# Zero matmuls in the idle time of TensorE, in a planned attention kernel with 32-row score matmuls

## The chip, the cores and the metric

The kernel runs on one core of a Trainium2 chip. The metric is the device time of one execution in microseconds, from the first to the last work on that core. Two runs of the kernel before are shown. The core has five engines that the text names by the profile's short names: PE (TensorE, matrix multiplication; PEld is its weight load), DVE (VectorE), ACT (ScalarE), POOL (GpSimd) and SP (SyncE, which issues the DMAs here).

## The reference: what is computed

The input x has 2048 tokens of 512 values in bfloat16. Four layers follow each other, A, B, A, B, each of them added to x, and each fed with a layer norm of x. A and B have their own weights, which both of their uses share.

```python
def _A_ref(x, wq, wk, wv, wo):          # 32 heads of 16, one key and one value head
    q = (x @ wq).reshape(B, S, H, Dh)   # per head
    k = x @ wk; v = x @ wv
    scores = einsum("bhqd,bkd->bhqk", q, k) * (Dh ** -0.5)
    o = einsum("bhqk,bkd->bhqd", softmax(scores), v)
    return o.reshape(B, S, H * Dh) @ wo

def _B_ref(x, wqkv, wo):                # linear attention, 32 heads of 16
    pq, pk = phi(q), phi(k)             # phi(t) = (t + 1 if t > 0 else exp(t)) + 1e-6
    kv = einsum("bhsd,bhse->bhde", pk, v); z = pk summed over s
    o = einsum("bhqd,bhde->bhqe", pq, kv) / (einsum("bhqd,bhd->bhq", pq, z) + 1e-6)
    return o.reshape(B, S, D) @ wo
```

The bulk of the work is A: for each of 32 heads a score matrix of 2048 by 2048, its exponential, and a product with 16 columns of values and one column of ones that gives the sum for the softmax.

## The kernel before, in words

**Scores.** A head has only 16 values, so a score matmul contracts over 16. The kernel gives it 32 rows of TensorE: queries of eight heads lie on the 128 partitions of `QT`, and the keys are repeated eight times down the partitions of `Kr`, in two copies. Copy `par` keeps the 16 rows of the even or the odd heads and has zeros in the others (`mpar` is the mask). A score matmul for head pair `j` (0 to 3) then reads the 32 partitions from 32 j on, of copy `par` and of the queries, and gives the scores of 128 keys by 512 queries of one head in one accumulator bank (`smm`, L569). Three score matmuls at different j can run side by side in TensorE.

**Positions.** The work of one A layer is a list of 2048 positions: a unit is a block of 512 queries, a group of eight heads and a copy (32 units), and a unit has 16 key tiles times 4 values of j. Each position is taken by one of two routes.

- The ACT route (`fill`, L668): three positions at a time, three score matmuls into one of two sets of three banks, one exponential by ACT over 1536 columns into a buffer of `PTA` (L689), then value matmuls.
- The DVE route (`dstep` and `dpass`, L704 and L744): one score matmul into bank 6, DVE turns it into an integer form (`xT`, L735); after two of them six DVE steps over 1024 columns make the exponential from the bits (`xu`, `xs`, L751 to L755) into a buffer of `PTD` (L756). This route works at least `LEAD` = 26 positions ahead.

**Values.** For each position four matmuls of 17 columns (`add_pv`, L583, issued at L608) use the exponentials as weights and add to columns 0 to 271 of bank 7. A unit has 64 such groups in bank 7. When the last is planned, DVE takes the reciprocal of the sums (`rden`, L620) and multiplies (`Osb`, L625). Bank 7 passes to the next unit after that. After the second copy of a head group, `Osb` is transposed (L793), copied to `OT` and, with all groups of a block, projected with `wo` and added to x.

**Mixed work.** When a block of 512 tokens of A is done, its layer norm, the B projections (`b_prep`, L823, all through the helper `proj`, L475) and `phi` are run while attention goes on with the next block. The rest of B (`b_main`, L876) runs tile by tile when A has ended, and in the first half of the kernel it is mixed with the projections for the next A.

**What sets the order.** Nothing is ordered by hand. A planner (`Sched`) runs a small model of the engines when the program is built. Each operation has a planned duration per engine, a priority, its inputs and the buffers it takes and gives back; whenever an engine is free in planned time (`run`, L180), the ready operation of best priority is appended to that engine's queue. Planned durations are for example 0.06 + 0.08 per score matmul (a set: 0.30 us), 0.22 for a score matmul of the DVE route, 0.15 for four value matmuls, 0.09 + 0.000833 per column for ACT (1.37 us for 1536), and 0.03 + 0.00036 per column for a projection matmul. The result is one fixed queue per engine, with semaphore waits where an operation needs another engine's result. On the chip nothing is reordered between the queues.

Buffers that the change touches: `NPA`, `NPD` (PTA and PTD, six each), `NE` (three exponentials of `phi`), `NO2` (three tiles in `b_main`).

Of the kernel before, what the change touches and what calls it, by code (L numbers as in the profile page):

```python
# [44 lines left out]
class Sched:  # L45


    def __init__(self, nc):
        self.nc = nc
        self.now = 0.0  # L50
        self.engs = [PE, AC, DV, PO, SP]
        self.tfree = {e: 0.0 for e in self.engs}
        self.pend = {e: [] for e in self.engs}
        self.ready = {e: [] for e in self.engs}
        self.order = {e: [] for e in self.engs}
        self.events = []
        self.seq = 0
        self.lastw = {}
        self.readers = {}
        self.all = []  # L60
        self.step = lambda now: False
        self.act_ok = lambda op: True
        self.ndma = 0

# [115 lines left out]
    def run(self):  # L180
        while True:
            go = True
            while go:
                go = self.step(self.now)
                for e in self.engs:
                    if self.tfree[e] <= self.now + 1e-9 and self._try(e):
                        go = True
            if not self.events:
                break
            t, _, f = heapq.heappop(self.events)  # L190
            self.now = max(self.now, t)
            if f is not None:
                f()
            while self.events and self.events[0][0] <= self.now + 1e-9:
                _, _, f = heapq.heappop(self.events)
                if f is not None:
                    f()
        left = [o for e in self.engs for (_, _, o) in self.ready[e] + self.pend[e] if not o.done]
        assert not left, [(o.name, o.engs) for o in left[:20]]
        STATS["end"] = max(o.vis for o in self.all)  # L200
# [112 lines left out]
def bass_interleave_layers__grouped_kv_mqa__linear_attn_block__prompt_kernel(  # L313
# [17 lines left out]
    LEAD = 26  # L331
    KC = 2

    xv = A_x.rearrange("b (t p) d -> p (b t) d", p=P)
# [6 lines left out]
    xnT = sb("xnT", [P, FT, S], BF16)  # L341
    NXN, NE = 3, 3
    xn_buf = sb("xn_buf", [P, NXN, D], BF16)
# [7 lines left out]
    mask8 = sb("mask8", [P, 8, 17], FP32)  # L351
    mpar = sb("mpar", [P, 2], FP32)
    wq_sb = sb("wq_sb", [P, FT, D], BF16)
# [6 lines left out]
    QT = sb("QT", [P, 2, NG, 512], BF16)  # L360
    Kr = sb("Kr", [P, 2, S], BF16)
    Vaug = sb("Vaug", [P, T, 20], BF16)
    NPA, NPD, NDX = 6, 6, 2
    PTA = sb("PTA", [P, NPA, 1536], BF16)
# [3 lines left out]
    xs = sb("xs", [P, NDX, 1024], FP16)  # L368
    Osb = sb("Osb", [P, 2, 4, D], BF16)
    OT = sb("OT", [P, 2, NG, 4, P], BF16)  # L370
# [7 lines left out]
    kvzbd = sb("kvzbd", [P, NG, 8 * 17], BF16)  # L378
    NO2 = 3
    Osb2 = sb("Osb2", [P, NO2, D], BF16)  # L380
# [31 lines left out]
    for c, (a, b) in enumerate(((0, 2), (2, 4), (4, 8), (8, 12), (12, 16))):  # L412
# [3 lines left out]
        if c == 1:  # L416
# [14 lines left out]
                                           fill=0.0, base=DH, channel_multiplier=-1), writes=["mask"], prio=1)  # L431
    add(DV, 0.1, lambda e: e.tensor_reduce(out=mpar[:], in_=mask8[:, :, 0:1].rearrange("p (a b) c -> p b (a c)", b=2),
                                           axis=mybir.AxisListType.X, op=ALU.add), reads=["mask"], writes=["mpar"], prio=2)
# [5 lines left out]

    state = {"layer": -1, "ctl": None}  # L440

# [40 lines left out]
    def k_proj(L, t0, n, prio):  # L482
        h = H_()
        a, b = t0 * P, (t0 + n) * P
        o = proj(h, [(wk_rep[:, ft, :], xnT[:, ft, a:b]) for ft in range(FT)], b - a, ["wkrep"] + [("xnT", t) for t in range(t0, t0 + n)], prio, name="kp")
        for m in range(2):
            def ev(e, m=m):
# [3 lines left out]
            if m == 0:  # L491
                ops = {}
            ops[m] = add((DV, AC), {DV: tdv(b - a), AC: tac(b - a)}, ev, deps=[o] + ([ops[0]] if m else []), uses=[h], rel=[h] if m else [],
                         reads=["mpar"], writes=[("K", m, t) for t in range(t0, t0 + n)], prio=prio - 0.05, name="kev")
# [32 lines left out]
    class Ctl:  # L527
# [25 lines left out]
        def ok(self, p):  # L553
            u, kt, j = self.pos[p]
            qb, g, par = self.units[u]
            a = self.have.get(("K", self.layer, par, kt))
            b = self.have.get(("Q", self.layer, qb, g))
            return a is not None and b is not None and a.done and b.done and a.vis <= sc.now + 0.05 and b.vis <= sc.now + 0.05
# [10 lines left out]
        def smm(self, e, p, b):  # L569
            u, kt, j = self.pos[p]  # L570
            qb, g, par = self.units[u]
            return e.matmul(bank(b), lhsT=Kr[32 * j:32 * j + 32, par, kt * P:(kt + 1) * P],  # L572
                            rhs=QT[32 * j:32 * j + 32, qb % 2, g, :], start=True, stop=True)

        def keys(self, ps_):
            r = []
            for p in ps_:
                u, kt, j = self.pos[p]
                qb, g, par = self.units[u]
                r += [("K", par, kt), ("QT", qb % 2, g)]  # L580
            return list(dict.fromkeys(r))

        def add_pv(self, p, src, hold, dep, last):  # L583
# [21 lines left out]
            def f(e):  # L605
                first = opened[0]
                for qs in range(4):
                    i = e.matmul(bank(7, 17, (qs * 4 + j) * 17), lhsT=src(qs), rhs=Vaug[:, kt, 0:17],  # L608
                                 start=(first and qs == 0), stop=(qs == 3), skip_group_check=True)
# [4 lines left out]
        def norm(self, u, last):  # L614
# [5 lines left out]
            o = add(DV, 0.246, lambda e: e.reciprocal(rden[:, hr.idx, :].unsqueeze(2), av[:, :, DH:DH + 1]), deps=[last], acq=[hr], uses=[h7], prio=0.0, name="recA")  # L620
            c0 = (8 * g + par) * DH
            ov_ = Osb[:, qb % 2, :, 128 * g:128 * (g + 1)].rearrange("p s (j r d) -> p s j r d", j=4, r=2)[:, :, :, par, :]

            def ml(e):
                return e.tensor_tensor(out=ov_, in0=bank(7, 272).rearrange("p (s j c) -> p s j c", s=4, j=4)[:, :, :, 0:DH],  # L625
                                       in1=rden[:, hr.idx, :].rearrange("p (s j) -> p s j", s=4).unsqueeze(3).to_broadcast([P, 4, 4, DH]), op=ALU.mult)
            o = add(DV, tdv(256), ml, deps=[o], uses=[h7, hr], rel=[h7, hr], writes=[("Osb", qb % 2, g, par)], prio=-0.01, name="mulA")
# [3 lines left out]
        def step(self, now):  # L631
            if self.layer is None:
                return False
            if self.ramp and all(self.have.get(("K", self.layer, m, t)) is not None and self.have[("K", self.layer, m, t)].done
                                 for m in range(2) for t in (0, T - 1)):
                self.ramp = False
# [4 lines left out]
            if self.pa >= n:  # L641
                self.tail = True
                self.layer_done()
                return False
# [59 lines left out]
        def dstep(self):  # L704
# [4 lines left out]
            while self.pd < n and self.taken[self.pd]:  # L709
                self.pd += 1  # L710
            if self.pd >= n or not self.ok(self.pd):
                return False
# [31 lines left out]
        def dpass(self, c):  # L744
            hx, hp = c["hx"], c["hp"]
            k = hx.idx
            lo = xT[:, k, :].bitcast(U16).rearrange("p (n two) -> p n two", two=2)[:, :, 0]
            pr = 3.0
            u_, s_ = xu[:, k, :], xs[:, k, :]
            kw = dict(uses=[hx], prio=pr)  # L750
            o = add(DV, tdv(1024, 0.52), lambda e: e.tensor_scalar(out=u_, in0=lo, scalar1=1.0 / 65536, scalar2=-0.5, op0=ALU.mult, op1=ALU.add), deps=c["p1"] + c["prev"], name="xu", **kw)  # L751
            o1 = add(DV, tdv(1024, 0.52), lambda e: e.tensor_tensor(out=s_, in0=u_, in1=u_, op=ALU.mult), deps=[o] + c["prev"], name="xsq", **kw)  # L752
            o2 = add(DV, tdv(1024, 0.26), lambda e: e.tensor_scalar(out=s_, in0=s_, scalar1=XK, scalar2=-XW, op0=ALU.mult, op1=ALU.add), deps=[o1], name="xw", **kw)  # L753
            o3 = add(DV, tdv(1024, 0.26), lambda e: e.tensor_scalar(out=u_, in0=u_, scalar1=1.0, scalar2=XL, op0=ALU.mult, op1=ALU.add), deps=[o1], name="xl", **kw)  # L754
            o4 = add(DV, tdv(1024, 0.52), lambda e: e.tensor_tensor(out=s_, in0=s_, in1=u_, op=ALU.mult), deps=[o2, o3], name="xc", **kw)  # L755
            o5 = add(DV, tdv(1024), lambda e: e.scalar_tensor_tensor(out=PTD[:, hp.idx, :].bitcast(U16), in0=xT[:, k, :], scalar=2.0 ** -9, in1=s_, op0=ALU.mult, op1=ALU.add),  # L756
                     deps=[o4] + c["prev"], uses=[hx, hp], rel=[hx], prio=pr, name="xo")
# [17 lines left out]

        def layer_done(self):
            if self.dcur is not None:
                raise AssertionError("open batch")

    ctl = Ctl()  # L780
    sc.step = ctl.step
    sc.act_ok = lambda op: ctl.ramp or ctl.tail
    banks.sets_for_misc = lambda: (1, 0) if (ctl.tail or (ctl.ramp and not (ctl.layer is not None and ctl.ok(0)))) else ((1,) if ctl.ramp else ())


    def epi_tr(L, qb, g):
# [3 lines left out]
        def tr(e):  # L790
            v = bank_bf(h.idx)
            for qs in range(4):
                i = e.transpose(v[:, qs, :], Osb[:, qb % 2, qs, g * P:(g + 1) * P], ident[:])  # L793
            return i
# [190 lines left out]
```

The softmax here doesn't subtract the row's maximum and nothing guards it: scores larger than these inputs give would overflow.

## Time and profile before

| | us |
|---|---|
| runs before | 1939.4 and 1934.91, median 1937.16 |
| the profiled execution | 1937.57, of which 1935.7 in the span from its first to its last instruction |
| exponentials by ACT (L689), 1179 of them | 1625.1 busy, 1464 ns each |
| score matmuls (L572), 4096 of 32 rows by 512 columns | 914.0 busy, 582 ns each |
| value matmuls (L608), 16384 of 17 columns, 14144 of them from PTA | 584.0 busy (PTA), 176 ns each |
| first DVE step (L735), 560 | 385.1 busy, 688 ns each |
| last DVE step (L756), 280 | 340.5 busy, 1216 ns each |
| mean granted clock of TensorE | 0.575 |

Durations are those of one profiled execution. Matmuls overlap each other, so a group's busy time is less than its count times its mean, and the time from one matmul's start to the next one's start says more than a duration. The profile's row of granted clock tells, in tenths, which part of TensorE's full clock its throttle let through: 1.0 is full and 0.5 half, and the records hold no other value here. "Idle before" is time in which an engine had nothing to do just before an instruction, with the engine that ended it.

By time, the span has these parts: the first layer norms, projections and a growing attention to about 50 us; attention of the first A to 900, from about 270 on with B's projections in it; the rest of B and the next projections to 1000; attention of the second A to about 1850, from about 1200 on with projections; the rest of the last B and the output to 1936.

### The profile page before, as it was taken

To read this page: it belongs to the slowest core of one execution; us is meant where nothing else is said; L and a number is where in the kernel's file an instruction comes from. 1 tells how busy PE (TensorE), PEld (TensorE's weight loads), DVE (VectorE), ACT (ScalarE), POOL (GpSimd) and SP (SyncE) were. 2 spreads that over 40 slices of the span, in tenths; PEclk is the share of its full clock that TensorE was granted. 3 is DMA by queue.
4 is the path that set the end of the run, shared out by engine and by line. 5 is a ranking of instruction groups with operands and counts; after the bars stand their busy time and mean duration, and the time that the engine had idled before them with its cause. 6 is when DMAs were issued, how large, how long until landed. Compare 5 with 4: busy or idle time off the path is not lost.

```text
span 1935.7 us, 49030 instructions
## 1 busy us (share of the span) xinstructions
PE 1778.2 (92%) x22208; PEld 820.9 (42%) x22208; DVE 1712.9 (88%) x3063; ACT 1702.0 (88%) x1330; POOL 45.1 (2%) x77
## 2 busy tenths in 40 slices
PE   7999999999999999998889999999999999997977
PEld 4444444444444444443444444444444444443434
DVE  7899989999889988887879999899898989985977
ACT  6999999999989999997589999999998999986973
POOL 2000000000000000000100000000000000000000
PEclk8555556555665555555975555655565555556559
DMA  3000000000000000000000000000000000000001
GB/s 110 2 1 2 2 1 2 2 2 2 1 2 2 2 1 2 2 2 2 1 2 2 2 2 2 2 2 2 1 2 1 2 1 2 2 2 1 2 1 44
DMA packets 7808, 10.50 MB, mean 5 GB/s; under 512 B 1456, under 2 KB 7088, under 8 KB 7600
## 3 DMA queue, kind: packets, MB, share of 16 engines
q1 hardware_dynamic: 7600, 7.37, 1.2%
q8 instruction: 173, 2.83, 0.6%
q14 instruction: 35, 0.29, 0.0%
HBM read 5.28 MB, written 2.10 MB: 4 GB/s over the span
## 4 chain that ended last, share of the span: by engine, by line
PE 57%; DVE 29%; ACT 11%; issue 1%; DMA 0%; POOL 0%; SPq 0%
PE ps_all L572 27%; PE ps_all L608 16%; PE ps_all L475 11%; ACT PTA L689 10%; DVE xT L735 8%; DVE PTD L756 6%; DVE xu L751 3%; DVE xs L755 2%; DVE xs L752 2%; DVE xu L754 1%; DVE xs L753 1%; PE ps_all L920 1%; DVE stats L444 1%; PE ps_all L458 1%; DVE x_sb L931 1%
## 5 line engine op out<-in xcount | busy, mean ns | idle before, releaser
L689 ACT ACTIVATE PTA<-ps_all 128x1536 bf16<-128x1536 f32 x1179 | 1625.1, 1464 | 117.7 <-PE ps_all L572 108.8
L572 PE MATMUL ps_all<-QT,Kr 32*128 32x512 bf16 x4096 | 914.0, 582 | 80.0 <-ACT PTA L689 38.8
L608 PEld LDWEIGHTS ps_all<-Vaug,PTA 128*128 128x128 bf16 x14144 | 470.3, 104 | 566.0 <-issue 552.6
L608 PE MATMUL ps_all<-Vaug,PTA 128*128 128x17 bf16 x14144 | 584.0, 176 | 4.6 <-ACT PTA L689 2.5
L735 DVE TENSOR_SCALAR xT<-ps_all 128x512 int32<-128x512 f32 x560 | 385.1, 688 | 116.1 <-PE ps_all L572 105.1
L756 DVE SCALAR_TENSOR_TENSOR PTD<-xT,xs 128x1024 uint16<-128x1024 int32 x280 | 340.5, 1216 | 1.1
L572 PEld LDWEIGHTS ps_all<-QT,Kr 32*128 32x128 bf16 x4096 | 160.0, 98 | 311.6 <-ACT PTA L689 152.6
L751 DVE TENSOR_SCALAR xu<-xT 128x1024 f16<-128x1024 uint16 x280 | 192.3, 687 | 3.1
L755 DVE TENSOR_TENSOR xs<-xs,xu 128x1024 f16<-128x1024 f16 x280 | 191.0, 682 | 1.4
L752 DVE TENSOR_TENSOR xs<-xu 128x1024 f16<-128x1024 f16 x280 | 190.4, 680 | 0.5
L608 PE MATMUL ps_all<-Vaug,PTD 128*128 128x17 bf16 x2240 | 111.6, 176 | 16.6 <-DVE Osb L625 8.0
L753 DVE TENSOR_SCALAR xs<-xs 128x1024 f16<-128x1024 f16 x280 | 116.4, 416 | 1.0
L754 DVE TENSOR_SCALAR xu<-xu 128x1024 f16<-128x1024 f16 x280 | 117.0, 418 | 0.0
L608 PEld LDWEIGHTS ps_all<-Vaug,PTD 128*128 128x128 bf16 x2240 | 86.1, 104 | 66.8 <-DVE Osb L625 26.9
L475 PE MATMUL ps_all<-wqkv_sb,xnT 128*128 128x512 bf16 x256 | 106.3, 559 | 2.6 <-ACT xnT L464 1.4
L448 POOL TENSOR_TENSOR rstd<-veps,mhalf 128x1 f32<-128x1 f32 x64 | 40.9, 643 | 1842.2 <-DVE veps L446 1623.6
L815 ACT ACTIVATE e_buf<-ps_all 128x512 f32<-128x512 f32 x64 | 37.8, 597 | 39.8 <-PE ps_all L475 38.7
L475 PE MATMUL ps_all<-xnT,wq_sb 128*128 128x512 bf16 x128 | 55.8, 566 | 4.4 <-DVE xT L735 2.1
L475 PE MATMUL ps_all<-xnT,wqkv_sb 128*128 128x512 bf16 x128 | 52.4, 545 | 6.5 <-DVE pqT L818 5.6
L475 PE MATMUL ps_all<-wo_sb,OT 128*128 128x512 bf16 x128 | 51.9, 543 | 2.9 <-ACT OT L799 1.4
L444 DVE BATCH_NORM_STATS2 stats<-x_sb 128x6 f32<-128x512 bf16 x64 | 43.2, 683 | 3.5 <-DMA x_sb<-in_A_x_dram 3.3
L458 PE MATMUL ps_all<-ident,xn_buf 128*128 128x128 bf16 x256 | 31.2, 267 | 15.3 <-DVE xn_buf L451 13.6
(64 smaller groups left out, 625.9 us busy)
## 6 DMA issues: line engine op xcount, KB each, us to landing
out_dram<-x_sb SPq DMA_DIRECT2D x16, 128.0 KB, 1.7
x_sb<-in_A_x_dram SPq DMA_DIRECT2D x3, 512.0 KB, 7.3
wqkv_sb<-in_B_wqkv_dram SPq DMA_DIRECT2D x1, 1536.0 KB, 11.3
x_sb<-in_A_x_dram SPq DMA_DIRECT2D x2, 256.0 KB, 3.5
wq_sb<-in_A_wq_dram SPq DMA_DIRECT2D x1, 512.0 KB, 5.5
wo_sb<-in_A_wo_dram SPq DMA_DIRECT2D x1, 512.0 KB, 8.5
wo_sb<-in_B_wo_dram SPq DMA_DIRECT2D x1, 512.0 KB, 10.9
wk_sb<-in_A_wk_dram SPq DMA_DIRECT2D x1, 16.0 KB, 2.7
```

The costliest lines, as they stand in the source:

```text
L444: add(DV, tdv(512), lambda e: e.bn_stats(stats[:, t, 0:6], x_sb[:, t, :]), reads=[("x", t)], writes=[("st", t)], prio=prio, name="bn")
L475: i = e.matmul(bank(h.idx, n), lhsT=l, rhs=r, start=(c + k == 0), stop=(c + k == len(mms) - 1))
L572: return e.matmul(bank(b), lhsT=Kr[32 * j:32 * j + 32, par, kt * P:(kt + 1) * P], rhs=QT[32 * j:32 * j + 32, qb % 2, g, :], start=True, st ...
L608: i = e.matmul(bank(7, 17, (qs * 4 + j) * 17), lhsT=src(qs), rhs=Vaug[:, kt, 0:17], start=(first and qs == 0), stop=(qs == 3), skip_group_ ...
L689: oe = add(AC, tac(m * 512), lambda e: e.activation(PTA[:, hp.idx, 0:m * 512], bank(3 * s, m * 512), ACTF.Exp, scale=SCALE), deps=[o] + pr ...
L735: o = add(DV, tdv(512), lambda e: e.tensor_scalar(out=xT[:, hx.idx, i * 512:(i + 1) * 512], in0=bank(6), scalar1=SCALE * LOG2E * 65536.0, ...
L751: o = add(DV, tdv(1024, 0.52), lambda e: e.tensor_scalar(out=u_, in0=lo, scalar1=1.0 / 65536, scalar2=-0.5, op0=ALU.mult, op1=ALU.add), de ...
L752: o1 = add(DV, tdv(1024, 0.52), lambda e: e.tensor_tensor(out=s_, in0=u_, in1=u_, op=ALU.mult), deps=[o] + c["prev"], name="xsq", **kw)
L753: o2 = add(DV, tdv(1024, 0.26), lambda e: e.tensor_scalar(out=s_, in0=s_, scalar1=XK, scalar2=-XW, op0=ALU.mult, op1=ALU.add), deps=[o1], ...
L754: o3 = add(DV, tdv(1024, 0.26), lambda e: e.tensor_scalar(out=u_, in0=u_, scalar1=1.0, scalar2=XL, op0=ALU.mult, op1=ALU.add), deps=[o1], ...
L755: o4 = add(DV, tdv(1024, 0.52), lambda e: e.tensor_tensor(out=s_, in0=s_, in1=u_, op=ALU.mult), deps=[o2, o3], name="xc", **kw)
L756: o5 = add(DV, tdv(1024), lambda e: e.scalar_tensor_tensor(out=PTD[:, hp.idx, :].bitcast(U16), in0=xT[:, k, :], scalar=2.0 ** -9, in1=s_, ...
```

## The change

Score matmuls keep 32 rows. The change writes the row count as a parameter (`RG` = 32, from which `NRG` = 4 groups of rows and `NM` = 2 copies of the keys follow), adds matmuls that compute nothing, and makes several buffers smaller.

The added matmul has the identity as weights (128 rows by 128 columns) and a tile of zeros, 240 columns, as the moving operand. It adds to columns 272 to 511 of bank 7, which nobody reads. The planner adds one when TensorE is free in planned time after all ready work was tried, in the main part of attention only (not while an A layer ramps up, and not after its last position was taken), only while a unit has some but not all of its 64 value groups in bank 7, and only as far as a credit allows that grows by `DUMMY` = 0.25 us per planned us, up to 2.0, and pays 0.1 for each. It waits for nothing but the identity and the zeros.

```diff
+    RG = 32
+    NRG, NM = P // RG, RG // DH
+    DUMMY = 0.25
...
-    NXN, NE = 3, 3
+    NXN, NE = 3, 2
...
-    NPA, NPD, NDX = 6, 6, 2
+    NPA, NPD, NDX = 5, 5, 2
...
-    Osb = sb("Osb", [P, 2, 4, D], BF16)
+    Osb = sb("Osb", [P, 2, NG, 4, P], BF16)
...
-    NO2 = 3
+    NO2 = 2
...
+    zer = sb("zer", [P, 240], BF16)
+    add(PO, 0.3, lambda e: e.memset(zer[:], 0.0), writes=["zer"], prio=4)
```

In the planner's loop, after the engines were tried:

```diff
+            if self.tfree[PE] <= self.now + 1e-9 and self.events:
+                self.idle(self.now)
             if not self.events:
                 break
```

The new function:

```diff
+    credit = [0.0, 0.0]
+
+    def idle(now):
+        if ctl.layer is None or ctl.ramp or ctl.tail or DUMMY <= 0:
+            credit[0], credit[1] = 0.0, now
+            return
+        credit[0] = min(2.0, credit[0] + (now - credit[1]) * DUMMY)
+        credit[1] = now
+        u = ctl.acc_owner
+        if credit[0] < 0.1 or u < 0 or not 0 < ctl.count[u] < 64:
+            return
+        credit[0] -= 0.1
+        o = add(PE, 0.11, lambda e: e.matmul(bank(7, 240, 272), lhsT=ident[:], rhs=zer[:], start=False, stop=True, skip_group_check=True),
+                reads=["ident", "zer"], prio=9.0, name="dummy")
+        sc._try(PE)
+
+    sc.idle = idle
```

The score matmul and the place of its result in bank 7, in terms of the parameters:

```diff
-            return e.matmul(bank(b), lhsT=Kr[32 * j:32 * j + 32, par, kt * P:(kt + 1) * P],
-                            rhs=QT[32 * j:32 * j + 32, qb % 2, g, :], start=True, stop=True)
+            i, m = (j % NRG, par * (4 // NRG) + j // NRG)
+            r = slice(i * RG, (i + 1) * RG)
+            return e.matmul(bank(b), lhsT=Kr[r, m, kt * P:(kt + 1) * P], rhs=QT[r, qb % 2, g, :], start=True, stop=True)
...
-                    i = e.matmul(bank(7, 17, (qs * 4 + j) * 17), lhsT=src(qs), rhs=Vaug[:, kt, 0:17],
+                    i = e.matmul(bank(7, 17, (qs * 4 + (j % NRG) * (4 // NRG) + j // NRG) * 17), lhsT=src(qs), rhs=Vaug[:, kt, 0:17],
```

`Osb` is stored with the head group before the token tile, and its writer and reader (L625, L793) follow. At the end of a layer the DVE route may close a batch of one position instead of two; `dpass` then works on 512 columns instead of 1024:

```diff
-            if self.pd >= n or not self.ok(self.pd):
+            if self.pd >= n:
+                if self.dcur is not None:
+                    self.dpass(self.dcur)
+                    self.dcur = None
+                return False
+            if not self.ok(self.pd):
                 return False
```

The loops over the copies of the keys (mask, evictions, checks whether a key tile is there) run over `NM` instead of 2. Two unused names are removed.

## The prediction

> **What bounds the kernel now.** I read the page first: busy shares, the 40 slices, the chain.
>
> ```profile
> PE 1778.2 (92%) x22208; PEld 820.9 (42%) x22208; DVE 1712.9 (88%) x3063; ACT 1702.0 (88%) x1330; POOL 45.1 (2%) x77
> ...
> PE   7999999999999999998889999999999999997977
> ...
> ACT  6999999999989999997589999999998999986973
> ...
> PEclk8555556555665555555975555655565555556559
> ...
> PE 57%; DVE 29%; ACT 11%; issue 1%; DMA 0%; POOL 0%; SPq 0%
> ```
>
> Three engines are near full, and TensorE, which carries 57% of the chain, is granted about half its clock wherever attention runs. So I asked for the engines' busy time by stage.
>
> ```profile
> 100.00:250.00 150.00, 139.79 (x1872) 64.26 (x1871) 145.37 (x246) 144.87 (x105) 0.00 (x0) 0.50 0.01 2
> 250.00:900.00 650.00, 614.05 (x7803) 278.48 (x7800) 588.06 (x1019) 600.29 (x452) 11.07 (x12) 0.55 0.01 2
> ...
> 1050.00:1200.00 150.00, 137.68 (x1857) 64.33 (x1856) 142.50 (x242) 142.79 (x105) 0.00 (x0) 0.50 0.01 2
> 1200.00:1850.00 650.00, 608.37 (x7588) 272.65 (x7586) 574.90 (x998) 586.52 (x440) 7.88 (x12) 0.55 0.01 2
> ```
>
> Columns: stretch, length, then busy of PE, weight loads, DVE, ACT, POOL, then granted clock. Where attention runs alone (100 to 250) ACT and DVE are 96.6% and 96.9% busy: they bind, even at half clock. Where the next layer's projections are mixed in, they fall to 88 to 92%. The list of waits for 250 to 900 says for whom:
>
> ```profile
> DVE xT L735 <- PE ps_all L572: 40.3, 75, 1.9
> ...
> ACT PTA L689 <- PE ps_all L572: 36.6, 52, 1.5
> ```
>
> There TensorE is late, and its clock is what can be bought. What does the clock follow? Its records change only at multiples of 3.413 us; four windows on that grid:
>
> ```profile
> 286.99:290.40 3.41, 3.41 (x35) 1.35 (x32) 3.00 (x5) 3.27 (x3) 0.00 (x0) 0.50 0.00 0
> 290.40:293.81 3.41, 3.41 (x35) 1.30 (x33) 2.98 (x7) 2.04 (x3) 0.00 (x0) 0.50 0.02 5
> 293.81:297.23 3.42, 2.95 (x38) 1.08 (x36) 3.42 (x7) 3.42 (x3) 0.00 (x0) 1.00 0.00 0
> 297.23:300.64 3.41, 3.04 (x60) 1.90 (x61) 3.41 (x9) 3.41 (x4) 0.93 (x1) 1.00 0.00 0
> ```
>
> The first two are both 100% busy, yet only the second is followed by full clock. Count the columns that each matmul streams, times its rows over 128: the first has 4912 score columns of 32 rows (a quarter: 1228) and 24 value matmuls of 17 (408), 1636 in all. The second swaps score columns for 2293 full-row projection columns: 456 + 408 + 2293 = 3157. The third has 3491 and is followed by full clock, the fourth (10 score matmuls 1280, 46 value matmuls 782, four transposes 512) has 2574 and is followed by half. I did this count for all 568 windows of the trace: below 2900 none of 457 is followed by full clock, above 3200 all 50, between them 30 of 61. A threshold near 3000 misplaces 9 windows; counting the 32-row matmuls whole, whatever the other weights, misplaces at least 59. So the gate looks at rows in use, not at whether TensorE is busy.
>
> The Trainium skill ("TensorE: Matmul & The Clock Gate", Part 1) says that a window of sustained activity opens the gate and an idle one closes it. From 48.1 us on the clock stood at 0.5 for 211.6 us, with TensorE busy 187.90 of the 200.62 us from 59.38 to 260.00 and never idle for a whole window: the measurement decides. By the page's rule the added matmuls would have nothing to repair and be pure load, the 2455 us below.
>
> **The change, part by part.** *Renaming.* With 32 rows a group, NRG is 4 and NM is 2; rows, mask and accumulator columns come out as before. Osb is laid out anew, but the multiply still writes runs of 16 and the transposes still read 128 columns: 0.
>
> *Buffers.* PTA and PTD go from 6 to 5. A PTA buffer lives from its scores to its last value matmul, some 3 us by the rows (0.54 + 1.46 + 0.42 and handovers) against one new buffer per 1.43 us: three suffice. Osb2/OT2 go from 3 to 2. At the end a tile holds its pair about 3.6 us (reciprocal at 1901.36 to last matmul 1904.75, the next three alike) and tiles follow every 1.88 us; two pairs allow one per 1.8 to 1.9, so 0 to +6 us, I take 4. In the middle tiles follow every 3.4 us: 0. The exponential's buffer goes from 3 to 2, off attention's path since one bank serves it there: 0 to +2, I take 1. Together +5.
>
> *Zero tile and tail.* One POOL memset (the Vaug memset took 168 ns) at the start, on a queue busy 2%: ahead of the others it could delay the first rstd by 0.2 us. A half batch for DVE at a layer's end: at most one per layer, under 5 us either way, taken 0.
>
> *The zero matmuls, how many.* The planner gives 0.25 us of credit per planned us and takes 0.1 for each: 2.5 per us at most. It also needs planned idle time. Between 100 and 250 there are 372 scores per 105 exponentials, 3.54 each. Planned TensorE work per exponential is 0.30 + 3 x 0.15 + 0.54 x (0.22 + 0.15) = 0.95 of 1.37 us; the idle 0.42 holds 3.8 matmuls of 0.11 us, so credit binds: 3.4. From 250 to 900, 222 projection matmuls over some 420 exponentials take another 0.11, transposes 0.03: 2.5. Over the two layers about 1000 + 2100 = 3100 (2500 to 4100).
>
> *What one costs.* No trace row shows it. 512 columns are spaced 427 ns at half clock and 216 at full (projection rows), so 240 columns take 200 or 101 ns; the identity's weights load beside them as those of the value matmuls do (27 ns apart). Switching row shapes costs extra: value to score rows 108 ns against 27, projection to score 567 against 427. So 0.10 to 0.16 us at full clock; I take 0.10, as most will stand beside 128-row work. They wait for nothing after the start. Behind each are the score group that ACT or DVE waits for and the value matmuls that free PTA.
>
> *What the rest of TensorE gains.* A score group to the values behind it, then the same at full clock:
>
> ```profile
> 292.73 0.61 PE L572 MATMUL ps_all<-QT,Kr 32*128 32x512 bf16 x3
> ...
> 293.27 0.49 PE L608 MATMUL ps_all<-Vaug,PTA 128*128 128x17 bf16 x12
> ...
> 294.22 0.39 PE L572 MATMUL ps_all<-QT,Kr 32*128 32x512 bf16 x3
> ...
> 294.54 0.46 PE L608 MATMUL ps_all<-Vaug,PTA 128*128 128x17 bf16 x12
> ```
>
> 0.54 against 0.32 us; twelve value matmuls to the next scores are 0.42 against 0.39. Per exponential with its DVE share TensorE needs 1.23 us at half clock and 0.88 at full; with projections 1.46 and 1.00. Adding the zeros: at full clock 0.88 + 0.34 = 1.22 and 1.00 + 0.25 = 1.25, under ACT's 1.37 to 1.43. At half clock 1.23 + 0.68 = 1.91 and 1.46 + 0.50 = 1.96, over it: TensorE would bind.
>
> *Does the gate stay open?* Attention's windows from 62 to 250 held 1789 on average (spread 329). At full clock and the pitch 1.40 the zeros add 3.4 x 240 x 3.413 / 1.40 = 1990: 3780, over the threshold by more than twice the spread. With projections 2175 (spread 535) + 1460 = 3640, and more as work moves faster. Once open it holds. Once shut, TensorE is full and its own slowness caps the count: (694 + 816) / 1.91 x 3.413 = 2700, so it needs a burst (projections, a stored run of up to 20 zeros), which by the spread comes in about one window in six alone and one in three with projections. A few per cent of dips, each a few windows long: I take 5% of the exponentials at half clock.
>
> *Do zeros count?* Transposes stream an identity, 127 of 128 values zero; left out, the count misplaces 15 windows instead of 9. So zeros seem to count. The same page (Part 4) says that transposes do not count as busy in the same way; then zeros might not, and the sum would again be 2455.
>
> *Sum.* Attention (50 to 900, 1000 to 1850) has 1700 us in which ACT and DVE are busy 1552 on average of the two (784 + 768). At the 96.75% of the undisturbed stretch that needs 1604: -96. Half clock for 5%: 1604 x 0.05 x (1.93 / 1.40 - 1) = +30. Buffers +5. 1935.7 - 96 + 30 + 5 = 1875, and 1.9 outside the span (1937.57 for that execution, the runs' median is 1937.16): **1877**.
>
> **Rivals.** *Shut gate, slower.* Zeros do not count, or the shut state holds. 3100 x 0.20 = 620 us go on a TensorE that has 108 us idle in attention: 1937.6 + 512 + 5 = 2455. For it: the shut count of 2700 lies below 3000. Against: the transposes, and the start, where the clock rises to 1.0 three times before 48 us. *Flickering.* The two states alternate. Each exponential at half clock costs 0.53 us more; the gain of 91 is gone at 15% of them, and at 37% the time is 2070. *Open but useless.* ACT and DVE wait for each other or for banks, not for TensorE; the two waits above would then be symptoms: 1925 to 1945.
>
> **How the numbers follow.** Gate mostly open: 0.60, 1825 (98% busy, no dips: -116) to 1905. Flickering 0.18, shut 0.17, useless 0.05. About 2% is what a measurement tells from no change: faster means under 1898, slower above 1976. Faster: 0.56 of the first case and 0.02 of flickering. Within 2%: 0.05 useless, 0.04 of the first, 0.08 of flickering. Slower: 0.08 and 0.17. The range runs from 1825 to 2070, which leaves out the shut gate and the worst flickering.
>
> **What would show it.** A clock row of 9s through attention; some 3100 new PE rows of 128x240 at about 0.1 us spacing; ACT near 97% from 250 to 900; the two waits on score matmuls under a third. A clock row still at 5 with those rows in it proves the shut gate. If the clock is 9 and ACT stays at 92%, my reading of the waits was wrong.

## The result: slower, with a clock that flickers

The changed kernel took 2042.26 and 2058.94 us, median 2050.6, against 1937.16 before: a ratio of 1.0586, 95% interval 1.0393 to 1.0778. The profiled execution took 2042.26, its span 2040.5. Ratios here and below leave out runs that took over 1.5% longer than the fastest of the same kernel. The forecast of 1877 was wrong in direction; the rival called flickering, in which the clock goes to and fro between its two values, is what happened.

The page of the changed kernel:

```profile
PE 1936.5 (95%) x25215; PEld 1004.5 (49%) x25215; DVE 1690.3 (83%) x3035; ACT 1717.3 (84%) x1337; POOL 44.9 (2%) x78
...
ACT  7878888998989988987478887898999999789873
...
PEclk9767767997978878867876776787989978569779
...
PE 66%; DVE 29%; ACT 3%; issue 1%; DMA 0%; POOL 0%; SPq 0%
...
L806 PE MATMUL ps_all<-zer,ident 128*128 128x240 bf16 x3007 | 564.8, 309 | 0.0
```

The mean granted clock rose from 0.575 to 0.798. There are 3007 zero matmuls (L806, called zeros below), and the value and score matmuls moved to L615 and L580. But ACT and DVE do the same work with a lower busy share, and TensorE carries more of the chain. By stage (columns as in the prediction):

```profile
100.00:250.00 150.00, 145.06 (x1866) 75.29 (x1866) 122.91 (x208) 125.12 (x90) 0.00 (x0) 0.70 0.01 2
250.00:900.00 650.00, 629.77 (x8571) 328.91 (x8569) 561.11 (x984) 580.99 (x438) 9.59 (x12) 0.82 0.01 2
1050.00:1200.00 150.00, 144.08 (x1820) 72.04 (x1818) 119.40 (x206) 124.44 (x95) 1.09 (x2) 0.71 0.01 2
1200.00:1850.00 650.00, 630.10 (x8450) 322.09 (x8449) 557.11 (x969) 576.32 (x429) 8.49 (x11) 0.80 0.01 2
```

The stretch from 100 to 250, where ACT and DVE were 97% busy at half clock, is hurt most: 83% and 82%, at a clock of 0.70. The list of waits over the whole span names TensorE:

```profile
ACT PTA L699 <- PE ps_all L580: 212.9, 326, 3.2
DVE xT L750 <- PE ps_all L580: 211.4, 242, 3.5
```

The same two waits before:

```profile
ACT PTA L689 <- PE ps_all L572: 108.8, 175, 4.6
DVE xT L735 <- PE ps_all L572: 105.1, 184, 1.9
```

Timing the units by the DVE reciprocal that ends each (`rden`) places the loss. "Units 0 to 9" runs here and below from the end of unit 0 to the end of unit 9, and "units 10 to 31" from there to the end of the last:

| us | before | changed |
|---|---|---|
| first A: units 0 to 9, units 10 to 31 | 239.9, 611.3 | 274.4, 633.4 |
| second A: units 0 to 9, units 10 to 31 | 243.7, 627.9 | 269.1, 640.9 |
| from the last unit of the first A to the first unit of the second | 96.7 | 105.3 |
| after the last unit | 59.7 | 62.2 |

95 of the span's 105 us are in the units.

**What the windows show.** I cut the trace on the 3.413 us grid again and counted, for each window, columns times rows over 128 (its sum), and the positions whose value matmuls started in it. The gate is called open in a window of full clock and shut in one of half clock. In the 381 windows of the changed kernel between 250 and 900 and between 1200 and 1850 the gate is open in 237 (62%). An open window does 8.43 positions, a shut one 6.02; before, the same stretches did 7.70, almost all at half clock. Between 60 and 250 and between 1050 and 1200 it is open in 41 of 100, with 8.61 positions open and 6.00 shut, against 8.38 before. So an open gate pays 9% where projections are mixed in, a shut one costs 22% there and 28% alone, and with projections the gate must be open 70% of the time to break even. Alone the open gate's 8.61 comes from 41 windows with a standard error near 0.4, so its 3% can't be told from nothing; taken as it stands, break-even is at 91%.

**Why it shuts.** Six windows in a row, zeros alone (columns: start and end, length, busy time and count of PE and of its weight loads, clock, DMA share and GB/s):

```profile
197.45:200.86 3.41, 0.94 (x6) 0.51 (x6) 1.00 0.00 0
200.86:204.27 3.41, 2.02 (x15) 1.23 (x15) 1.00 0.02 5
204.27:207.69 3.42, 0.00 (x0) 0.00 (x0) 1.00 0.00 0
207.69:211.10 3.41, 0.76 (x3) 0.28 (x3) 0.50 0.00 0
211.10:214.51 3.41, 1.56 (x6) 0.56 (x6) 0.50 0.02 5
214.51:217.93 3.42, 1.80 (x9) 1.10 (x10) 0.50 0.00 0
```

The zeros come in runs: 15 in the second window (its sum is 5093) and none in the third (1941), and after the third the gate is shut. TensorE's timeline of that third window:

```profile
203.55 0.67 PE L806 MATMUL ps_all<-zer,ident 128*128 128x240 bf16 x5
204.16 0.39 PE L580 MATMUL ps_all<-QT,Kr 32*128 32x512 bf16 x3
204.48 0.36 PE L615 MATMUL ps_all<-Vaug,PTA 128*128 128x17 bf16 x8
204.77 0.60 PE L580 MATMUL ps_all<-QT,Kr 32*128 32x512 bf16 x4
206.08 0.56 PE L615 MATMUL ps_all<-Vaug,PTA 128*128 128x17 bf16 x16 [0.71 <-DVE Osb L632]
206.68 0.60 PE L580 MATMUL ps_all<-QT,Kr 32*128 32x512 bf16 x4
207.21 0.36 PE L615 MATMUL ps_all<-Vaug,PTD 128*128 128x17 bf16 x8
207.43 0.46 PE L615 MATMUL ps_all<-Vaug,PTA 128*128 128x17 bf16 x12
207.74 0.76 PE L806 MATMUL ps_all<-zer,ident 128*128 128x240 bf16 x3
```

Bank 7 changes hands here, which is called a boundary below: the unit's last value matmuls start at 204.48, then TensorE waits for DVE's multiply (L632), then it works off a pile of value matmuls. The planner bars zeros from a unit's last value group to the next unit's first, and none stands in the pile either: 3.5 us without one, longer than a gate window. Of the 237 open windows with projections, 57 hold the reciprocal of a boundary or follow one by at most 1.5 us. They hold 565 columns of zeros on average, the other 180 hold 1771, and the sums are 3046 against 4108. Of the 57, 26 (46%) are followed by a shut gate; of the 180, 11 (6%).

### The profile page after: what moved, and what is told of

Read it like the earlier page. It is cut to its first block, busy times and chain, and to the rows that moved or that the text cites. A ratio compares the mean times of both kernels' runs of the same rounds, so it can differ in the third digit from the quotient of the medians.

```text
span 2040.5 us, 55033 instructions
## 1 busy us (share of the span) xinstructions
PE 1936.5 (95%) x25215; PEld 1004.5 (49%) x25215; DVE 1690.3 (83%) x3035; ACT 1717.3 (84%) x1337; POOL 44.9 (2%) x78
## 4 chain that ended last, share of the span: by engine, by line
PE 66%; DVE 29%; ACT 3%; issue 1%; DMA 0%; POOL 0%; SPq 0%
PE ps_all L580 23%; PE ps_all L615 18%; PE ps_all L806 15%; PE ps_all L481 7%; DVE xT L750 6%; DVE PTD L772 5%; DVE xu L767 3%; DVE xs L771 3%; DVE xs L768 3%; ACT PTA L699 3%; DVE xu L770 2%; DVE xs L769 2%; PE ps_all L949 2%; DVE Osb L632 1%; DVE stats L450 1%
## 5 line engine op out<-in xcount | busy, mean ns | idle before, releaser
L699 ACT ACTIVATE PTA<-ps_all 128x1536 bf16<-128x1536 f32 (+1 forms) x1183 | 1646.2, 1472 | 222.5 <-PE ps_all L580 212.9
L580 PE MATMUL ps_all<-QT,Kr 32*128 32x512 bf16 x4096 | 746.0, 455 | 31.5 <-ACT PTA L699 14.5
L615 PEld LDWEIGHTS ps_all<-Vaug,PTA 128*128 128x128 bf16 x14172 | 454.6, 99 | 394.2 <-issue 377.5
L615 PE MATMUL ps_all<-Vaug,PTA 128*128 128x17 bf16 x14172 | 572.9, 173 | 9.3 <-DVE Osb L632 8.0
L806 PE MATMUL ps_all<-zer,ident 128*128 128x240 bf16 x3007 | 564.8, 309 | 0.0
L772 DVE SCALAR_TENSOR_TENSOR PTD<-xT,xs 128x1024 uint16<-128x1024 int32 (+1 forms) x277 | 336.3, 1214 | 0.6
L580 PEld LDWEIGHTS ps_all<-QT,Kr 32*128 32x128 bf16 x4096 | 158.5, 94 | 362.0 <-issue 165.9
L806 PEld LDWEIGHTS ps_all<-zer,ident 128*128 128x128 bf16 x3007 | 264.9, 106 | 79.3 <-issue 51.5
L767 DVE TENSOR_SCALAR xu<-xT 128x1024 f16<-128x1024 uint16 (+1 forms) x277 | 189.9, 685 | 3.0
L771 DVE TENSOR_TENSOR xs<-xs,xu 128x1024 f16<-128x1024 f16 (+1 forms) x277 | 189.1, 683 | 1.6
L768 DVE TENSOR_TENSOR xs<-xu 128x1024 f16<-128x1024 f16 (+1 forms) x277 | 188.2, 680 | 0.4
L615 PE MATMUL ps_all<-Vaug,PTD 128*128 128x17 bf16 x2212 | 109.3, 173 | 19.6 <-DVE Osb L632 16.6
L769 DVE TENSOR_SCALAR xs<-xs 128x1024 f16<-128x1024 f16 (+1 forms) x277 | 115.2, 416 | 0.7
L770 DVE TENSOR_SCALAR xu<-xu 128x1024 f16<-128x1024 f16 (+1 forms) x277 | 115.7, 418 | 0.0
L615 PEld LDWEIGHTS ps_all<-Vaug,PTD 128*128 128x128 bf16 x2212 | 83.9, 99 | 58.6 <-DVE Osb L632 28.9
```

Source lines behind the costliest of these rows:

```text
L580: return e.matmul(bank(b), lhsT=Kr[r, m, kt * P:(kt + 1) * P], rhs=QT[r, qb % 2, g, :], start=True, stop=True)
L615: i = e.matmul(bank(7, 17, (qs * 4 + (j % NRG) * (4 // NRG) + j // NRG) * 17), lhsT=src(qs), rhs=Vaug[:, kt, 0:17], start=(first and qs == ...
L699: oe = add(AC, tac(m * 512), lambda e: e.activation(PTA[:, hp.idx, 0:m * 512], bank(3 * s, m * 512), ACTF.Exp, scale=SCALE), deps=[o] + pr ...
L767: o = add(DV, tdv(w, 0.52), lambda e: e.tensor_scalar(out=u_, in0=lo, scalar1=1.0 / 65536, scalar2=-0.5, op0=ALU.mult, op1=ALU.add), deps= ...
L768: o1 = add(DV, tdv(w, 0.52), lambda e: e.tensor_tensor(out=s_, in0=u_, in1=u_, op=ALU.mult), deps=[o] + c["prev"], name="xsq", **kw)
L769: o2 = add(DV, tdv(w, 0.26), lambda e: e.tensor_scalar(out=s_, in0=s_, scalar1=XK, scalar2=-XW, op0=ALU.mult, op1=ALU.add), deps=[o1], nam ...
```

## The experiments

Where no ratio is given, a kernel was run once. The first four part the causes. **No zeros**, all else of the change kept:

```diff
-    DUMMY = 0.25
+    DUMMY = 0.0
```

> The changed kernel with its credit at 0, so that no zero matmul is issued; the smaller buffers and all renaming stay. Gate theory (the loss comes from zero matmuls that run while the clock gate is shut): 1930 to 1950 us, the clock near 0.57, ACT and DVE near 96% busy between 100 and 250 us. Rival (the smaller buffers stall ACT and DVE): 2000 us or more, with the wait of ACT on score matmuls still above 150 us.

1943.47 us, ratio 1.0017 (1.0003 to 1.0032), clock 0.566. The buffers, the new layout and the tail together cost some 3 us. Its stretch of pure attention, by stage, is that of before to a tenth:

```profile
100.00:250.00 150.00, 139.76 (x1876) 64.58 (x1875) 145.35 (x247) 144.84 (x106) 0.00 (x0) 0.50 0.01 2
```

**Old buffers**, with the zeros:

```diff
-    NXN, NE = 3, 2
+    NXN, NE = 3, 3
...
-    Vaug = sb("Vaug", [P, T, 20], BF16)
-    NPA, NPD, NDX = 5, 5, 2
+    Vaug = sb("Vaug", [P, T, 18], BF16)
+    NPA, NPD, NDX = 6, 6, 2
...
-    NO2 = 2
+    NO2 = 3
```

> The changed kernel with the buffers of before (6 PTA, 6 PTD, 3 for the exponential of phi, 3 in the last stage; the value tile has 18 instead of 20 columns to make room). Gate theory: within 1% of the changed kernel, 2030 to 2055 us, clock 0.78 to 0.82. Rival (buffers): back to 1900 to 1940 us.

2029.06 us, ratio 1.046 (1.042 to 1.0499), clock 0.804, a microsecond under the stated range. More buffers may help a little beside zeros (the intervals overlap), but they are not the loss.

**Zeros of 32 rows**:

```diff
-... lhsT=ident[:], rhs=zer[:], ...
+... lhsT=ident[0:32, :], rhs=zer[0:32, :], ...
```

> The same number of zero matmuls of 240 columns, but with 32 rows instead of 128. Gate theory (rows in use count): each adds 60 instead of 240 to a window, the sums of attention windows stay below 3000, the clock falls back to 0.57 to 0.62, and the 3007 matmuls cost up to 0.2 us each on an engine that is full: 2250 to 2450 us. Rival (the gate watches whether TensorE is busy): clock near 0.80 and 2030 to 2070 us, as in the changed kernel.

2303.54 us, clock 0.553. From its page:

```profile
PE 2231.0 (97%) x25215; PEld 1118.3 (49%) x25215; DVE 1711.7 (74%) x3035; ACT 1763.9 (77%) x1337; POOL 44.7 (2%) x78
...
L806 PE MATMUL ps_all<-zer,ident 32*128 32x240 bf16 x3007 | 742.7, 387 | 0.0
```

The same 3007 matmuls of 240 columns keep TensorE 97% busy, and the gate is shut as much as before the change: the clock is 0.50 between 100 and 250 us and 0.53 between 250 and 900. Rows in use open it, busy time doesn't. The run also gives the price of these zeros behind a gate that is mostly shut: 360 us over the run without zeros.

**Weights in place of zeros**:

```diff
-... rhs=zer[:], ...
+... rhs=wq_sb[:, 0, 0:240], ...
```

> The same matmuls with a slice of the query weights as moving data instead of zeros, into the same unread columns. Gate theory: data does not matter, 2030 to 2070 us, clock 0.78 to 0.82. Rival (zeros count less than data): the sums of a window rise, clock above 0.88 and less than 1980 us.

2041.11 us, clock 0.802, against 2042.26 and 0.798. For the gate the data made no difference.

**The boundary, in the plan.** In these two the planner keeps a list of planned columns (`sc.recent()` is the sum of the last 3.4 planned us), and score sets can bring zeros of their own, into the bank that they overwrite next. `NEED` is 3300 and `NZ` is 3:

```diff
+            if not self.ramp:
+                nz = max(0, min(NZ, -(-(NEED - sc.recent() - 384) // 240)))
...
+                for _ in range(nz):
+                    e.matmul(bank(3 * s, 240), lhsT=ident[:], rhs=zer[:], start=True, stop=True)
```

> The changed kernel, and in planning a score set (3 matmuls) up to 3 more zero matmuls of 240 columns are put in front of it, into a bank that the set is about to overwrite, whenever the planned columns times rows/128 of the last 3.4 planned us are under 3300. These are possible while bank 7 is handed from unit to unit, where the changed kernel has none. Theory A (the gate shuts at unit boundaries, where zeros are barred for some 3 us): open-to-shut transitions fall to less than half of the 51 in attention, clock 0.88 or more, 1880 to 1960 us. Theory B (zeros come in runs everywhere, the boundary is one cause of many): clock 0.80 to 0.86, 1980 to 2050 us.

> As the boundary run, and an idle-time zero matmul is added only while those planned columns of the last 3.4 us are under 3300 (credit 0.4 instead of 0.25 per us). Theory A: 2000 to 2800 zero matmuls instead of 3007, spread more evenly, clock 0.88 or more, 1850 to 1940 us. Theory B: clock below 0.86 and 1960 us or more.

2071.45 us at a clock of 0.788, and 2161.02 at 0.652. The first missed both ranges; the second missed theory A and lies in the open-ended range of theory B. The boundary run had 360 zeros before score sets, but the planned list looks back: it is full of zeros just issued when the boundary begins. Its open windows at a boundary held 963 columns of zeros instead of 565, yet their sum rose only from 3046 to 3148, and 27 of 60 were still followed by a shut gate (elsewhere 6 of 165). Adding zeros by need took away the surplus (2113 zeros) and with it the margin: open windows between 250 and 900 held 3298 instead of 3898 and half of them were followed by a shut gate. These two runs decided nothing about the boundary.

**64 rows**, without zeros and with a smaller credit:

```diff
-    RG = 32
+    RG = 64
-    DUMMY = 0.25
+    DUMMY = 0.0        # the second run: 0.1
```

> No zero matmuls, but score matmuls of 64 rows (four masked copies of the keys instead of two; two of a set of three can run side by side instead of three). Rows-in-use theory: a score matmul counts 256 instead of 128, attention windows alone hold about 2900 at full clock, with projections 3400, so the clock flickers between 0.65 and 0.9 with nothing added; TensorE needs about 1.15 us per exponential at full clock and 1.75 at half: 1890 to 2030 us. Rival (the gate watches busy time, or the zeros themselves): clock 0.57 as before, 2150 us or more.

> 64-row score matmuls and the change's zero matmuls at a credit of 0.1 per us, about 1200 to 1600 of them. Rows-in-use theory: sums about 3700 in attention, the gate is open except at unit boundaries, clock 0.88 or more, 1850 to 1930 us. Rival (any added TensorE work is lost): slower than the 64-row run without zeros by 100 us or more.

2105.35 us at 0.684, and 2076.64 at 0.835 with 1604 zeros. The clock of the first answers as rows in use say, with nothing added, and the thresholds that divide the windows of the two runs best are 3052 and 3007. The second's clock stayed under the stated 0.88, and both times missed their ranges. With two score matmuls side by side instead of three, TensorE does 7.05 positions in a shut window of pure attention against 8.40 before. The rival of pure load asked for 2205 us or more in the second run, and 2076.64 refutes it; that zeros make this kernel faster isn't shown by one run of each.

**Where zeros cost** (the words behind `#` here and below name the run and are not in the code):

```diff
-        if credit[0] < 0.1 or u < 0 or not 0 < ctl.count[u] < 64:
+        if credit[0] < 0.1 or u < 10 or not 0 < ctl.count[u] < 64:               # late units
+        if credit[0] < 0.1 or u < 0 or u >= 10 or not 0 < ctl.count[u] < 64:     # early units
```

> Zero matmuls only in units 10 to 31 of each A layer, where projections are mixed in; none in units 0 to 9, where attention runs nearly alone. In the changed kernel units 0 to 9 took 274 and 269 us against 240 and 244 before, and units 10 to 31 633 and 641 against 611 and 628. Theory (alone, ACT and DVE bind even at half clock, so an open gate buys nothing there and a shut one costs): units 0 to 9 return to 240 to 247 us each, the later ones stay within 10 us of the changed kernel, 1975 to 2000 us. Rival (the loss is spread with the number of zeros, 2061 of 3007): about 2015 us, with units 10 to 31 carrying most of it.

> The complement: zero matmuls only in units 0 to 9 (954 of them). Theory: units 0 to 9 stay at 265 to 280 us, the later ones return to 605 to 630 us, 1990 to 2015 us. Rival (loss by number of zeros): 1970 to 1975 us.

Late units: 1967.42 us, ratio 1.0151 (1.0116 to 1.0187); units 0 to 9 took 240.3 and 244.7, units 10 to 31 627.4 and 633.7. The units are as stated, the whole is 8 us under its range. Early units: 2032.03, 17 us over its range; units 0 to 9 273.3 and 286.0, the others 612.0 and 637.9. So 954 zeros cost more than 2061: the loss goes by place, not by number. Where attention runs alone the zeros only lose. That the second A of the early run is slower than stated stays unexplained; it is one profile.

**Half the credit, and a wider gap**:

```diff
-    DUMMY = 0.25
+    DUMMY = 0.125                                                                # half
-        if credit[0] < 0.1 or u < 0 or not 0 < ctl.count[u] < 64:
+        if credit[0] < 0.1 or u < 0 or not 6 < ctl.count[u] < 58:                # gap
```

> Half the credit (0.125 per us; 2013 zero matmuls by the plan). Theory: the planned order has the gate's threshold of 3000 columns missed in 40% instead of 16% of its 3.41 us stretches, so the clock falls to 0.64 to 0.74, and each zero then costs 0.2 us more often: 2010 to 2070 us, no better than the full dose. Rival (loss in proportion to the number of zeros): 2000 to 2012 us at an unchanged share of open windows.

> Zero matmuls barred for the first 6 and the last 6 of a unit's 64 value groups as well, which widens the stretch without them at each unit boundary (2517 by the plan). Theory A (boundaries shut the gate): 55 or more of 64 boundaries are followed by a shut gate, clock 0.68 to 0.76, 2030 to 2090 us in spite of 490 fewer zeros. Theory B (boundaries do not matter, the number of zeros does): clock 0.78 to 0.80, 2000 to 2035 us.

Half: 2051.2 us at a clock of 0.700, with 2013 zeros: two thirds of the zeros, all of the loss. Gap: 2093.18 us at 0.740, with 490 fewer zeros. After 60 of the 64 reciprocals a shut window follows within two, against 48 in the changed kernel. This is as theory A said, the time 3 us over its range, but the run doesn't part the wider bar from the smaller number of zeros, since fewer zeros alone lower the clock too, as the run at half the credit shows. The next runs part them.

**Holding the gate.** The last three put zeros also behind value matmuls, in the same instruction group, whenever the last 3.4 planned us (`HZ`) hold too few columns. `LOWP` is the bound on these columns, `NZP` the most zeros behind one group, and `U0` the first unit that gets any:

```diff
...
+                    if not self.ramp and not self.tail and u >= U0 and self.count[u] < 63:
+                        extra[0] = max(0, min(NZP, -(-(LOWP - sc.recent(HZ) - 68) // 240)))
+                    o.dur = {PE: 0.15 + 0.11 * extra[0]}
...
+                for _ in range(extra[0]):
+                    i = e.matmul(bank(7, 240, 272), lhsT=ident[:], rhs=zer[:], start=False, stop=True, skip_group_check=True)
```

> Zero matmuls only in units 10 to 31 (as in the late-units run), and there, besides the change's own, up to 2 behind each value group and up to 3 before each score set whenever the planned columns of the last 3.4 planned us are under 3450. The plan's own order then misses 3000 columns in 6.5% of these units' 3.41 us stretches (changed kernel 15.6%). Theory (only the gate's holding failed): gate open in 80% or more of the windows of units 10 to 31, these units 590 to 612 us each against 627 and 634 in the late-units run, 1905 to 1940 us in all. Rival (the zeros fill TensorE and an open gate pays nothing): open as above but 620 us or more, 1960 us or more in all.

> As the run before, with up to 3 zeros behind a value group under 3300 columns and zeros before a score set only under 2000; the plan misses 7.5%. Theory: 590 to 615 us per set of units 10 to 31, 1905 to 1945 us. Rival: 620 us or more, 1960 us or more.

> Top-up in all units, up to 2 behind a value group and 3 before a score set under 3600 columns; the plan misses 6% in units 0 to 9 and 4% in units 10 to 31, and has TensorE busier. Theory: gate open in 85% or more of attention, units 0 to 9 245 to 260 us (against 274 and 269 in the changed kernel), units 10 to 31 605 to 625, 1925 to 1970 us. Rival: units 0 to 9 270 us or more, 2020 us or more.

The first took 2008.86 us (four runs from 1986.43 to 2053.09; ratio 1.0367, 1.0329 to 1.0405), the second 2031.81 (1992.26 to 2047.44; 1.0353, 1.0265 to 1.0441) and the third 2099.36. Units 10 to 31 took 624.5 and 653.8 us in the first, 650.9 and 660.9 in the second, 655.6 and 661.8 in the third, whose units 0 to 9 took 276.2 and 289.6. All three theories fell. The rivals' times came true, but not the open gate that the first two rivals took for granted, and the clock's own records say why. The table has the windows between 250 and 900 and between 1200 and 1850 us:

| | open share | an open window is followed by shut | a shut one by open |
|---|---|---|---|
| changed kernel | 62% | 16% (37 of 237) | 26% (38 of 144) |
| late units | 62% | 17% (40 of 236) | 28% (41 of 145) |
| top-up, late units | 60% | 8% (19 of 230) | 13% (20 of 151) |
| top-up, late units, second | 54% | 14% (29 of 204) | 18% (31 of 177) |
| top-up, all units | 61% | 6% (14 of 233) | 10% (15 of 148) |

The first top-up also settles what a boundary does. Against the late-units run it has 2223 zeros instead of 2061, but they stand elsewhere: its open windows at a boundary hold 1298 columns of zeros instead of 534, their sums are 3366 instead of 2940, and 9 of 51 of them are followed by a shut gate instead of 27 of 57. Away from boundaries it is 10 of 179 against 13 of 179. So it was the boundaries without zeros that shut the gate, and zeros there mostly keep it open. (This compares one profile of each.)

But the first and the third top-up halved the openings along with the closings. Behind a shut gate TensorE is full (busy without a break in the three shut windows shown above) and works through a fixed order at its own pace; what then opens the gate is a window that happens to hold much more than the mean. In the changed kernel shut windows hold 2683 with a spread of 480, in the third top-up some 2585 with a spread of 280. An even order has few windows over 3000, so both states last longer, and the share stays. This is read from the counts; no run changed the spread behind a shut gate by itself. Each open share is close to openings / (openings + closings): 26 / (26 + 16) = 62%, 13 / (13 + 8) = 62%. In the all-units run an open window also does less (7.75 and 7.33 positions in the two stretches): the zeros themselves fill TensorE. No version here beats the kernel before. In the profiles from the late-units run on, 115 to 129 of the 768 projection matmuls of 512 columns have no record, so their windows' sums (2585, 3366 and 2940 above) are a little low; score, value and zero matmuls are all there.

## Why the prediction failed, by its steps

- **The lists of waits:** the two rows that the prediction shows as 250 to 900 are those of 270 to 900; from 250 on they are 40.7 and 38.5 us, which changes nothing.
- **Renaming, buffers, tail (+5 us):** right. All of it without zeros is +0.17%, some 3 us.
- **How many zeros (3100):** right, 3007.
- **What one costs (0.10 or 0.20 us):** right. Zeros that follow each other at one clock start 102 ns apart when the gate is open and 200 when it is shut. The last zero of a run costs more: scores start 198 and 340 ns behind it, against 103 and 108 behind a value matmul.
- **What opens the gate:** right. In the changed kernel no window under 2900 (of 205) is followed by an open gate and every one over 3200 (of 309) is; the best threshold, 3043, misplaces 21 of 597, and if zeros are counted as nothing the best one misplaces 156. The kernel before, the run without zeros, the zeros of 32 rows and the two kernels with 64 rows all give 3007 to 3052. On transposes the Trainium skill ("TensorE: Matmul & The Clock Gate", Part 4) is not borne out: left out, 37 are misplaced, in full 21. (The profile lists this kernel's transposes as plain matmuls with the identity.)
- **The gain of an open gate (-96 us):** the mechanism was right. At the rate of open windows the 1152 positions of units 1 to 9 of both layers and the 2816 of units 10 to 31 would take 1152 / 8.61 x 3.413 + 2816 / 8.43 x 3.413 = 1597 us against 1722.8 before, -126 (with no gain in units 1 to 9, -114). This is an estimate from open windows; no run held the gate open through a layer. That the rate isn't that of a backlog is shown by the first top-up: the 111 windows with projections that stand at least eight windows into an open stretch did 8.43 positions too, with ACT 99% busy and DVE 95%.
- **"Does the gate stay open?":** this step failed. It took "a few per cent of dips", 5% of the exponentials at half clock, +30 us. Measured: an open window is followed by a shut one in 16% of cases with projections and 27% without (11 of 41). 203 of 481 windows are shut, and 34% of the positions fall in them. By the estimate above the term is 1817.8 - 1597 = 221 us instead of 30; -126 + 221 is the +95 of the units. Two things were wrong in it. The spread was taken from the kernel before (329 to 535), as if the zeros were spread evenly and the other work kept its spread: in the 278 open windows of the changed kernel the sums spread by 923, the zeros by themselves by 910 and the rest by 853. And the bar on zeros while bank 7 changes hands, which stands in the diff, was never set against the length of a gate window: 26 of the 37 closings in the table are at boundaries.
- **The shut state's own hold:** the sum of 2700 behind a shut gate was right in size (2576 and 2669 measured in the two stretches of the first A), and so was one opening in six alone (10 of 59). It was used only as the length of a dip, not as the second half of a balance in which openings weigh as much as closings.
- **The flickering rival:** right, and its price nearly so: 1847 + 0.34 x 607 = 2053 us for 34% of the exponentials, against 2042.26 in the execution from which the 34% is. Some of that is luck, since both the gain of an open gate (96 against 126) and the cost of a shut one (206 against 221) came out too small. It had been given 0.18.

## What to carry to other kernels

The mean of a window's sum isn't enough for a gate with a threshold: ask for the spread of the fixed order itself, and look for every place where the filler, work that computes nothing, is barred for as long as one window. Where filler work runs on the engine that the gate slows down, compute both states: one that is faster only while open, and slower than before while shut, needs an open share before it pays (here some 70% with projections and 91% or more alone, against 62% and 41% reached). And fill only where the engine is the bound: where ACT and DVE bound at half clock, the filler only lost (240 us became 274).

## What the runs showed of the hardware that was not expected

- In the ten kernels with complete records (before, changed, and the runs up to 64 rows), 3267 windows under 2900 full-row columns per 3.413 us were never followed by full clock and 2073 over 3200 always, with score matmuls of 32 or 64 rows and zeros of 32 or 128. The Trainium skill's rule for this gate ("TensorE: Matmul & The Clock Gate", Part 1) speaks of a busy window; here a window at 100% busy with 1636 such columns was followed by a shut gate.
- All-zero moving data counts as full work for the gate, and data in its place changed nothing (clock 0.798 and 0.802, 2042 and 2041 us).
- Zeros spread more evenly made the shut state last as well as the open one: in two of the three top-up runs closings fell from 16% to 8% and 6%, and openings from 26% to 13% and 10%.
